# Spreading the stores of the last output tile over SyncE, ScalarE and GpSimd, at the end of an attention and feed-forward kernel

## Chip, cores, metric

One core of a Trainium2 chip. The metric is device time in microseconds (us), measured around the whole program; the span in a profile, from the first to the last instruction, is about 1.8 us shorter. "Tail" below means the time from the end of the last eviction on VectorE to the end of the span.

## The reference

Attention with an extra exp(-m) in the denominator, on (8, 12, 448, 64) queries, keys and values, followed by a feed-forward layer with a maximum over three products:

```python
scores = scale * q @ k.T;  m = max(scores);  e = exp(scores - m)
attn = e / (sum(e) + exp(-m) + 1e-9);  x = attn @ v          # to (3584, 768)
h = max(x @ w1, x @ w2, x @ w3);  out = h @ w_out            # (3584, 768) float32
```

## The kernel before

TensorE works almost without a gap from the first scores to the last output tile. An output tile is 128 tokens by 768 columns, made in pieces of columns: six matmuls into PSUM, one eviction by VectorE into `o_sb`, and then one store for each half of 64 partitions, since the two halves go to different rows. (An ordinary tile's first piece is stored together with its second.) Only the cuts of the very last tile differ.

```python
def out_piece(bp, t, c, w, queues):
    ...
    nc.vector.tensor_scalar(out=o_sb[:, c : c + w], in0=op_ps[:, 0:w],
                            scalar1=1.0 / LAMBDA, scalar2=None, op0=ALU.mult)
    if queues is None:
        return
    for half in range(2):
        ...
        queues[half].dma_start(out=rows[:, outs[1] : c + w],
                               in_=o_sb[half * HP : half * HP + HP, outs[1] : c + w])
    outs[1] = c + w
```

GpSimd issues all loads of the kernel but two (they convert to fp16 on the way, and are written by software on GpSimd): 108 transfers. It also copies V into its working layout. Its last such work:

```python
if 5 <= i + 1 < NI:
    prep_v(i + 1, nc.gpsimd)      # last time for i = NI - 2, near 260 us
...                               # cut: shift_q, load_more, the end of the loop
for pr in range(NP):              # the last heads, then the last feed-forward batch
    finish = av(NI - 1, NI % NEB, pr, "EO")
```

After the last line of the program each engine gets closing instructions: SyncE waits for all transfer semaphores, and a barrier ends the program.

The softmax here doesn't subtract the row's maximum and nothing guards it: scores larger than these inputs give would overflow.

Of the kernel before, what the change touches and what calls it, by code (L numbers as in the profile page):

```python
# [21 lines left out]
def kernel(  # L22
# [11 lines left out]
    nc = tc.nc  # L34
# [468 lines left out]
    NW = DM // 2  # L503
# [40 lines left out]
            pieces.append((up_piece, (b, fcs, i, q0, qn), NDC * w * (qn + 6)))  # L544

    def add_out(b):
        sy, sc = nc.sync, nc.scalar
        for t in range(0, 3) if b % 2 == 0 else range(3, 7):
            cuts = [(0, NW, None), (NW, NW, (sy, sy))]
            if b == B - 1 and t == 6:  # L550
                cuts = [(0, NW, (sy, sy)), (NW, 256, (sc, sc)), (NW + 256, 128, (sy, sc))]
            for c, w, queues in cuts:
                pieces.append((out_piece, (b // 2, t, c, w, queues), NFC * (w + 6)))

    def add_batch(b):
        add_up(b, 0, S, [(i, fc) for fc in range(NFC) for i in range(3)])
        add_out(b)
# [120 lines left out]
    for i in range(3, NI):  # L678
# [6 lines left out]
        for vi, units in enumerate(visits):  # L685
# [17 lines left out]
            if vi == 2 and first:  # L703
                x_transpose_pe(i - 1, "E")
                fill(per / 2)
                prep_v(i, DV)
                for w, cols in ((0, (0, NE)), (1, (0, NE)), (2, (NE, NO)), (2, (0, NE))):
                    add_up(0, *cols, [(w, f) for f in (0, 2, 4)])
                add_out(0)
                per = share(n)  # L710
# [59 lines left out]
```

## Time and profile before

| before | us |
|---|---|
| time, median of 3 runs | 338.64 (338.59 to 338.93) |
| span of the profile | 336.88 |
| end of the last eviction | 331.92 |
| last store landed | 335.60 |
| SyncE's closing waits done | 336.05 |

The prediction shows the busy shares, the chain and the last stores. The profile lists instructions by engine (count, then shortest, median and longest in ns, then first and last start in us).

### The profile page before, as it was taken

How to read it: one execution, taken by the hardware profiler on the slowest of the kernel's cores; microseconds unless marked ns; L12 is line 12 of the kernel's file. 1: busy time of each engine (PE TensorE's matmuls, PEld its weight loads, DVE VectorE, ACT ScalarE, POOL GpSimd, SP SyncE). 2: the span in 40 equal slices, each digit the busy share in tenths (PEclk: the TensorE clock that was granted, in tenths of full speed). 3: DMA queues.
4: the chain of work that ended last, by engine and by line, in shares of the span. 5: the costliest groups of instructions: out<-in, count | busy, mean ns of one | idle time of the engine just before them, and what ended most of it. 6: DMA issues, size and time to landing. Idle time of an engine off the chain costs nothing.

```text
span 336.9 us, 10248 instructions
## 1 busy us (share of the span) xinstructions
PE 326.1 (97%) x4316; PEld 195.9 (58%) x4316; DVE 199.9 (59%) x521; ACT 183.1 (54%) x289; POOL 146.7 (44%) x260
## 2 busy tenths in 40 slices
PE   7899999999999999999999999999999999999993
PEld 3668788866556655565546646555556555565552
DVE  4556675566566556556656556556556556575552
ACT  4768856655665755676556655666565665420000
POOL 8596578880671539170854328351754000000000
PEclk9999999999999999999999999999999999999999
DMA  8999999799799999969996999989990730124016
GB/s 141 197 200 207 203 205 191 128 161 191 109 108 132 171 234 145 124 96 190 177 156 81 114 259 120 150 99 220 186 149 18 164 89 2 31 47 129 0 33 157
DMA packets 84815, 46.46 MB, mean 138 GB/s; under 512 B 53280, under 2 KB 81312, under 8 KB 84768
## 3 DMA queue, kind: packets, MB, share of 16 engines
q0 software_dynamic: 29120, 21.80, 48.6%
q1 hardware_dynamic: 55264, 23.60, 41.3%
q8 instruction: 34, 0.56, 0.7%
q10 hardware_dynamic: 384, 0.39, 0.4%
q14 instruction: 13, 0.11, 0.1%
HBM read 44.04 MB, written 11.01 MB: 163 GB/s over the span
## 4 chain that ended last, share of the span: by engine, by line
PE 87%; DMA 5%; ACT 2%; DVE 2%; issue 1%; POOL 1%; POOLq 0%; ACTq 0%
PE p_i L490 48%; PE op_ps L514 14%; PE stp L304 11%; PE avp L388 9%; DMA xT<-xn 3%; ACT e L324 2%; DMA ld_q<-in_q_dram 2%; PE avp L344 2%; PE avp L361 1%; DVE xn L404 1%; PE trT L229 1%; DVE QT L190 1%; PE xtp L463 0%; ACT QT L188 0%; DVE rb L401 0%
## 5 line engine op out<-in xcount | busy, mean ns | idle before, releaser
L324 ACT ACTIVATE e<-stp 128x896 f16<-128x896 f32 (+4 forms) x171 | 143.9, 901 | 60.3 <-PE stp L304 60.1
L490 PE MATMUL p_i<-xT,w 128*128 128x448 f16 (+2 forms) x972 | 173.1, 332 | 0.5 <-DMA xT<-xn 0.3
L490 PEld LDWEIGHTS <-w 128*128 128x128 f16 x972 | 90.2, 98 | 69.1 <-issue 6.0
L249 POOL COPY QT<-QT 64x384 f16<-64x384 f16 (+1 forms) x84 | 46.9, 558 | 93.9 <-DMA QT<-ld_q 69.2
L501 DVE TENSOR_TENSOR hT<-hT,p_i 128x448 f16<-128x448 f16 (+2 forms) x96 | 59.7, 622 | 35.7 <-PE p_i L490 35.6
L514 PE MATMUL op_ps<-w,hT 128*128 128x384 f16 (+2 forms) x342 | 58.5, 323 | 0.0
L304 PE MATMUL stp<-QT,KT 64*64 64x448 f16 (+2 forms) x756 | 48.1, 338 | 2.6 <-ACT e L324 0.9
L499 DVE CAST hT<-p_i 128x448 f16<-128x448 f32 (+2 forms) x48 | 30.0, 625 | 25.2 <-PE p_i L490 25.2
L514 PEld LDWEIGHTS <-hT 128*128 128x128 f16 x342 | 32.0, 98 | 22.4 <-issue 2.0
L424 ACT ACTIVATE xn<-end,rl 64x64 f16<-64x64 f32 x72 | 24.9, 346 | 34.5 <-DVE rl L421 34.1
L521 DVE TENSOR_SCALAR o_sb<-op_ps 128x384 f32<-128x384 f32 (+2 forms) x57 | 31.2, 547 | 17.4 <-PE op_ps L514 16.8
L388 PE MATMUL avp<-vx,e 128*128 128x65 f16 x936 | 38.6, 194 | 0.0
L388 PEld LDWEIGHTS <-e 128*128 128x128 f16 x936 | 32.1, 97 | 2.3
L304 PEld LDWEIGHTS <-KT 64*64 64x64 f16 x756 | 15.8, 105 | 26.8 <-issue 23.9
L398 DVE TENSOR_SCALAR rb<-avp 128x6 f32<-128x6 f32 (+2 forms) x54 | 8.8, 164 | 36.8 <-PE avp L388 36.8
L404 DVE TENSOR_TENSOR xn<-avp,rb 128x384 f16<-128x384 f32 (+2 forms) x54 | 29.3, 543 | 1.8
L433 POOL COPY vx<-ld_v 128x768 f16<-128x768 f16 x21 | 17.2, 820 | 6.8 <-issue 4.2
L344 PEld LDWEIGHTS <-e 64*64 64x64 f16 x624 | 13.7, 107 | 8.1 <-issue 1.7
L102 POOL DMA_DIRECT2D ld_q<-in_q_dram x24 | 17.4, 723 | 2.3 <-DMA w<-in_moe_w_dram 1.1
L102 POOL DMA_DIRECT2D ld_k<-in_k_dram x24 | 17.3, 722 | 2.1 <-DMA w<-in_moe_w_out_dram 1.1
L414 ACT ACTIVATE end<-avp 128x65 f32<-128x65 f32 x36 | 8.2, 227 | 17.1 <-PE p_i L490 12.4
L115 POOL DMA_DIRECT2D ld_v<-in_v_dram x24 | 15.2, 634 | 2.6 <-DMA w<-in_moe_w_dram 1.3
(52 smaller groups left out, 162.1 us busy)
## 6 DMA issues: line engine op xcount, KB each, us to landing
out_dram<-o_sb SPq DMA_DIRECT2D x54, 192.0 KB, 4.0
ld_v<-in_v_dram POOLq DMA_DIRECT2D x48, 128.0 KB, 5.1
ld_k<-in_k_dram POOLq DMA_DIRECT2D x23, 224.0 KB, 6.6
ld_q<-in_q_dram POOLq DMA_DIRECT2D x23, 224.0 KB, 7.5
w<-in_moe_w_dram POOLq DMA_DIRECT2D x9, 384.0 KB, 9.2
w<-in_moe_w_out_dram POOLq DMA_DIRECT2D x3, 384.0 KB, 8.5
xT<-xn SPq DMA_TRANSPOSE x18, 4.8
QT<-ld_q SPq DMA_TRANSPOSE x17, 7.3
```

Source lines behind the costliest of these rows:

```text
L102: nc.gpsimd.dma_start(out=tiles[nm][:, 1 : NP * T + 1].rearrange("x (r t) d -> x r (t d)", r=NP)[:, p0:p1], in_=src[:, p0:p1],)
L249: eng.tensor_copy(out=t[d0 : d0 + HP, o * 128 : (o + n) * 128], in_=t[s0 : s0 + HP, a * 128 : (a + n) * 128],)
L304: nc.tensor.matmul(out=stp[half * HP : half * HP + HP, par, j * qn : (j + 1) * qn], lhsT=k_block(i, pr, h2, x[half]), rhs=q_cols(i, pr, h2 ...
L324: nc.scalar.activation(out=dst, in_=src, func=AF.Exp, scale=scale)
L388: nc.tensor.matmul(out=ps[:, hh, j * D1 : (j + 1) * D1], lhsT=eF[:, o : o + 128], rhs=vx[:, 2 * pr + hh, (x[0]), 0:D1], start=False, stop= ...
L404: nc.vector.tensor_tensor(out=xn[i][:, pr, ws[0] : ws[0] + nw].rearrange("p j h d -> p h j d"), in0=acc[:, :, :, 0:D], in1=rb.unsqueeze(3) ...
L424: nc.scalar.activation(out=xn[i][0:HP, pr, 3, hh], in_=end[h, 0:D], func=AF.Copy, scale=rl[h])
L490: nc.tensor.matmul(out=p_i[:, j * qn : (j + 1) * qn], lhsT=w_sb[i][:, dc, ts(fc, 128)], rhs=xT[b][:, dc, q0 : q0 + qn], start=(dc == 0), s ...
L499: nc.vector.tensor_copy(out=dst, in_=src)
L501: nc.vector.tensor_tensor(out=dst, in0=dst, in1=src, op=ALU.max)
L514: nc.tensor.matmul(out=op_ps[:, 0:w], lhsT=hT[bp][:, fc, ts(t, 128)], rhs=wout_sb[:, fc, c : c + w], start=(fc == 0), stop=(fc == NFC - 1),)
L521: nc.vector.tensor_scalar(out=o_sb[:, c : c + w], in0=op_ps[:, 0:w], scalar1=1.0 / LAMBDA, scalar2=None, op0=ALU.mult,)
```

## The change

The intent: SyncE issues the last tile's pieces one after another and is late with the last; ScalarE is busy with three issues; GpSimd is idle. So the halves of the 384-column piece go to SyncE and ScalarE, both halves of the 256-column piece to GpSimd, and the last 128 columns stay on SyncE and ScalarE.

```diff
     def add_out(b):
-        sy, sc = nc.sync, nc.scalar
+        sy, sc, gp = nc.sync, nc.scalar, nc.gpsimd
         for t in range(0, 3) if b % 2 == 0 else range(3, 7):
             cuts = [(0, NW, None), (NW, NW, (sy, sy))]
             if b == B - 1 and t == 6:
-                cuts = [(0, NW, (sy, sy)), (NW, 256, (sc, sc)), (NW + 256, 128, (sy, sc))]
+                cuts = [(0, NW, (sy, sc)), (NW, 256, (gp, gp)), (NW + 256, 128, (sy, sc))]
```

## The prediction

> **What bounds the kernel now.** I read the busy shares first, then the chain of waits that ended last, then the last ten microseconds of the timeline and each output store's issue and landing.
>
> ```profile
> PE 326.1 (97%) x4316; PEld 195.9 (58%) x4316; DVE 199.9 (59%) x521; ACT 183.1 (54%) x289; POOL 146.7 (44%) x260
> ```
>
> TensorE is busy 97% of 336.9 us. The granted clock is 0.999. Nothing in the change touches TensorE; a comparison of the two programs finds its 8634 rows and VectorE's identical. So 331.5 of the 336.9 us cannot move, and the whole question lies after the last matmul. There the chain in order of time ends as follows (start, length, what):
>
> ```profile
> 323.55 8.06 PE op_ps L514 x54
> 331.61 0.02 issue
> 331.63 0.29 DVE o_sb L521
> ```
>
> The last eviction ends at 331.92, yet the span ends at 336.88. These 4.95 us are the tail: stores, their landing and the closing barrier. The timeline of that stretch (start, length, engine, what; a merged line begins at the first and ends with the last of its group):
>
> ```profile
> 330.49 1.43 DVE L521 TENSOR_SCALAR o_sb<-op_ps 128x384 f32<-128x384 f32 x3 [0.42 <-DMA out_dram<-o_sb]
> 332.28 1.70 SPq L531 DMA_DIRECT2D out_dram<-o_sb  x2
> 331.60 1.84 ACTq L531 DMA_DIRECT2D out_dram<-o_sb  x3
> ```
>
> The three VectorE evictions are the last tile's 384, 256 and 128 columns, ending at 331.05, 331.57 and 331.92. ScalarE issues at 331.60, 332.19 and 332.89. SyncE issues the previous tile's second half at 330.62, then the 384-column halves at 331.32 and 332.28, and the last piece only at 333.51, 1.59 us after its data was ready. That last store alone, as the trace lists it, followed by the one before it:
>
> ```profile
> L531 SPq DMA_DIRECT2D out_dram<-o_sb x1: 466/466/466, 333.5 to 333.5; - x1
> DMA to landing us min/median/max: 2.1/2.1/2.1
> ...
> L531 SPq DMA_DIRECT2D out_dram<-o_sb x1: 803/803/803, 332.3 to 332.3; - x1
> ```
>
> It lands at 333.51 + 2.09 = 335.60. ScalarE's last lands at 332.89 + 2.52 = 335.41, SyncE's second half at 332.28 + 2.53 = 334.81. From 335.60 to the end are 1.28 us of closing waits and barriers. So the tail is: 1.59 us of SyncE running late, 2.09 us of one store, 1.28 us of closing.
>
> The transfer engines are the second limit in this stretch (columns as in the heading; last two are busy share and GB/s):
>
> ```profile
> core 0: us, PE busy (x) PEld busy (x) DVE busy (x) ACT busy (x) POOL busy (x), PEclk, DMA share, GB/s
> 331.00:332.00 1.00, 0.60 (x7) 0.32 (x5) 0.77 (x3) 0.00 (x0) 0.00 (x0) 1.00 0.80 172
> 332.00:333.00 1.00, 0.00 (x0) 0.00 (x0) 0.00 (x0) 0.00 (x0) 0.00 (x0) 1.00 0.83 250
> 333.00:334.00 1.00, 0.00 (x0) 0.00 (x0) 0.00 (x0) 0.00 (x0) 0.00 (x0) 1.00 0.93 244
> 334.00:335.00 1.00, 0.00 (x0) 0.00 (x0) 0.00 (x0) 0.00 (x0) 0.00 (x0) 1.00 0.49 129
> ```
>
> They are 80 to 93% busy until 334, so earlier issues cannot be turned wholly into earlier landings. GpSimd does nothing at all there; its last work was at 260.
>
> **What the Trainium skill says.** "DMA: Bandwidth & Descriptors", section "Issuing engines are not separate DMA queues": "Initiating DMAs on multiple engines concurrently will only save the time on the sequencer it takes to initiate the DMA". The trace agrees that there is such a time: SyncE needs 0.47 to 0.59 us for each store when alone.
>
> "Perfetto Trace Analysis", section "DMA Instruction — HWDGE (DVE, Sync)": the hardware descriptor generator is shared by the issuing sequencers, locked for one of them, and the profiled length of an issue includes the wait for that lock. The trace fits: SyncE's two 384-column issues, made while ScalarE issues, take 0.92 and 0.80 us, not 0.47 to 0.59.
>
> "DMA: Bandwidth & Descriptors", section "Specifications": first byte after about 1 us from GpSimd, about 0.6 us from SyncE or ScalarE. The trace is slower in both: first packets about 1.33 us after an isolated GpSimd issue, 1.12 to 1.21 us after SyncE's or ScalarE's.
>
> "SBUF — State Buffer", section "Who interferes with whom": VectorE in a two-port mode locks GpSimd out. I expect nothing of it here: the evictions of 384 and 128 columns take 557 and 292 ns, so (557 - 292)/256 = 1.04 ns a column, which is no doubled rate, and only one, of 0.29 us, is left when GpSimd starts.
>
> **The change part by part.**
>
> 1. The second half of the 384 columns leaves SyncE for ScalarE. SyncE loses one issue of 0.80 us, plus some 0.43 us between it and the last one. Its last issue is then bounded by the data (331.92) or by the end of the first half's issue: 331.32 + 0.47 to 0.92 = 331.8 to 332.2. I put it at 332.0 to 332.4, in place of 333.51. ScalarE issues its half at 331.08, as soon as the 384 columns are evicted, done at about 331.65; that store moves 1.2 us forward.
>
> 2. ScalarE loses its two 256-column issues (0.55 and 0.60 us). Its last 128 columns can go at 331.95 in place of 332.89. Some waiting for the shared generator remains, as four issues still fall within a microsecond, so 332.0 to 332.5. With 2.1 to 2.5 us to landing, SyncE's and ScalarE's last stores land at 334.1 to 335.0.
>
> 3. GpSimd gains two stores of 64 KB. Data ready at 331.57, first issue about 331.62. The nearest kin in the trace are the pairs of V loads, also 64 partitions: 0.63 and 0.64 us of GpSimd for an issue, 3.2 us from issue to landing when other traffic is absent. Those read 256 KB each and convert it; a 64 KB store needs about 1.33 us to its first packet, 0.3 us of packets, and about 0.6 us until the semaphores are full, so about 2.3 us, and I allow 2.3 to 3.2. Second issue at 332.25, landing at 334.6 to 335.4. This is likely the new last one, and it is on the path.
>
> 4. The bytes do not change. From 331.2 on, two tiles' worth (the last two), 786 KB, are moved. At 260 GB/s, a little above the 244 to 250 of the full stretches, that takes 3.0 us, so the last packet goes at about 334.2 at the earliest, against 334.9 now. As the last landing now comes 0.7 us after the last packet, it cannot be before about 334.9. This is an estimate from those rates, and it caps the gain at 0.7 us.
>
> 5. Closing: SyncE goes through all the queues' semaphores in a fixed order, about 0.06 us each. With another one last, that may cost or save up to 0.4 us. I take none.
>
> Sum: the last landing moves from 335.60 to about 335.0 (between part 4's floor and the late end of part 3). 338.64 - 0.6 = 338.0 us, a gain of 0.2%.
>
> **Rivals.** First, GpSimd's path is the new bound and eats everything: at 3.2 us from the second issue it lands at 335.45, and with a slower start of the software path or transfer contention at 336 or a little later. For: loads under traffic took 4 us and more. Against: they are bigger and ran against full queues. Time 338.5 to 339.2.
>
> Second, the transfer engines do not matter and only the issue does: SyncE's last store issues 1.2 us earlier, the closing order helps too, and the gain is 1.2 to 1.4 us: 337.3. For: the last store takes only 2.09 us in all. Against: the busy share of 0.8 to 0.93.
>
> Third, the generator lock stays the bound: ScalarE's early half now collides with SyncE's previous-tile store and with the next one, each issue takes 0.8 to 0.9 us, and SyncE's last goes at 333.0. That would make 338.1 or so, close to my number for another reason.
>
> **Range and chances.** The whole tail that the change can reach is 1.59 us of waiting in SyncE, 0.5% of the time; even removing it entirely and saving in the closing would not come to 2% (6.8 us). A loss of 6.8 us would need a GpSimd store of some 10 us. So "within 2%" is nearly certain. The three runs of before span 0.34 us, so noise is half of the expected gain. Range 337.3 to 338.8.
>
> **What would show it.** Right: SyncE's last store is issued at or before 332.5; ScalarE's first at about 331.1; GpSimd's two at 331.6 and 332.25 with about 0.63 us each; the last landing near 335.0 and belonging to GpSimd; TensorE unchanged up to 331.5. Wrong: GpSimd's landing after 335.6, SyncE's issues still at 0.8 to 0.9 us and its last one after 333, or a closing stretch longer than the 1.28 us, for instance because the end must wait for GpSimd's queue in another way.

## More of the kernel before

```profile
L765 POOLq DRAIN  x3: 45/93/5048, 260.0 to 336.6; - x3
L765 SPq DRAIN  x3: 7/7/7, 336.0 to 336.4; - x3
```

GpSimd has three closing drains. One takes 5048 ns, and the first starts at 260.0: as soon as GpSimd ran out of work. It was over at 265, 72 us before the end, and cost nothing. SyncE's drains take 7 ns.

## The result

The changed kernel took 340.00 us (median of 4 runs, 339.81 to 340.81), the kernel before 338.62 in the same comparison. The ratio is 1.0046, 95% interval 1.0026 to 1.0066: 0.46% slower, 1.6 us, where 0.6 us of gain was predicted. (Ratios are the mean time of one kernel's fast runs over that of the other's of the same rounds, so not quite the ratio of the medians.) Within 2%, as forecast, but outside the stated range.

The profiled run of after is the longest of its four: span 338.95. Its last eviction ends at 332.46, 0.54 us later than before; that difference was there before GpSimd's last copy, at 260 us, is done, where the two programs are the same. The tail is 338.95 - 332.46 = 6.49 us against 4.95: 1.54 us more, which is the loss.

The chain that ended last, after (start, length, what):

```profile
331.69 0.44 DVE o_sb L521
332.12 0.28 issue
332.41 0.56 POOL out_dram L531
332.96 0.56 POOLq L765
```

In the kernel before the chain ended with the last eviction of 128 columns. Now it goes from the 256-column eviction to GpSimd's first store, and then to line 765 on GpSimd's sequencer: not to a transfer, but to a closing instruction. Which one, the view of the closing instructions tells:

```profile
L765 SPq EVENT_SEMAPHORE  x11: 17/28/2045, 333.8 to 338.9; - x11
L765 POOLq DRAIN  x3: 51/93/5315, 332.9 to 338.7; - x3
L765 SPq DRAIN  x3: 7/7/7, 336.3 to 338.4; - x3
```

The long drain is the same one as before, 5.3 instead of 5.0 us, but it now starts at 332.86 in place of 260, since GpSimd's last work is the two stores. It ends at 338.18. SyncE had all transfers landed and its own drains begun at 336.33, and then stood at the barrier for 1.85 us. (SyncE's longest wait, 2045 ns, lies before that. By the semaphore that it names it is for GpSimd's second store: it ends at 335.86, 0.02 us after that store has landed, and SyncE needs another 0.47 us for the rest of its fixed order. So GpSimd's store also set when SyncE was done.)

The stores themselves, in the timeline of after:

```profile
330.64 3.06 SPq L531 DMA_DIRECT2D out_dram<-o_sb  x4
331.62 1.35 ACTq L531 DMA_DIRECT2D out_dram<-o_sb  x2
332.41 1.12 POOL L531 DMA_DIRECT2D out_dram<-o_sb  x2 [71.28 <-DVE o_sb L521]
```

SyncE's last store now goes 0.77 us after the last eviction, in place of 1.59. But it lands at 3.57 us after it, in place of 3.67: the gain of 0.8 us in the issue became 0.1 us in the landing. That store alone, as the trace lists it (it was issued at 333.24):

```profile
L531 SPq DMA_DIRECT2D out_dram<-o_sb x1: 466/466/466, 333.2 to 333.2; - x1
DMA to landing us min/median/max: 2.8/2.8/2.8
```

The transfer engines are the likely reason why there was little to win (last two columns: busy share and GB/s):

```profile
332.00:333.00 1.00, 0.14 (x3) 0.00 (x0) 0.40 (x2) 0.00 (x0) 0.59 (x2) 1.00 0.98 255
333.00:334.00 1.00, 0.00 (x0) 0.00 (x0) 0.00 (x0) 0.00 (x0) 0.52 (x1) 1.00 0.99 242
334.00:335.00 1.00, 0.00 (x0) 0.00 (x0) 0.00 (x0) 0.00 (x0) 0.00 (x0) 1.00 0.84 231
```

From 332 to 334 they are 98 to 99% busy, at about the rate of before (242 to 255 GB/s, against 244 to 250). No run tests this reading alone, and it is no fixed limit: in pairs, below, the same bytes had landed 3.29 us after the last eviction.

### The profile page after: what moved, and what is told of

It is laid out like the page before. It is cut to its first block, busy times and chain, and to the rows that moved or that the text cites. A ratio compares the mean times of both kernels' runs of the same rounds, so it can differ in the third digit from the quotient of the medians.

```text
span 339.0 us, 10249 instructions
## 1 busy us (share of the span) xinstructions
PE 326.6 (96%) x4316; PEld 196.2 (58%) x4316; DVE 198.9 (59%) x521; ACT 183.0 (54%) x289; POOL 147.8 (44%) x262
## 4 chain that ended last, share of the span: by engine, by line
PE 89%; DVE 3%; DMA 3%; ACT 3%; issue 1%; POOLq 0%; POOL 0%; ACTq 0%
PE p_i L490 48%; PE op_ps L514 14%; PE stp L304 11%; PE avp L388 9%; DMA xT<-xn 3%; ACT e L324 2%; PE avp L344 2%; PE warm L175 1%; PE avp L361 1%; DVE xn L404 1%; DVE QT L190 1%; PE trT L229 1%; ACT QT L188 1%; PE trT L213 1%; PE xtp L463 0%
## 5 line engine op out<-in xcount | busy, mean ns | idle before, releaser
L531 POOL DMA_DIRECT2D out_dram<-o_sb x2 | 1.1, 560 | 71.3 <-DVE o_sb L521 71.3
```

## The experiments

Theory: GpSimd's closing drain, some 5 us after its last work, now sets the end. Rivals: the early ScalarE issue slows SyncE's and ScalarE's stores; the drain waits for GpSimd's stores to land, so it is the stores and not the drain; the drain's length is for what gathered up since the start, not for the late stores.

All runs gave correct results. On the chips that these runs got, the times of the kernel before spread over 3.9 to 5.7 us within a job, which swamps half a microsecond. In the profiled runs such differences lie before GpSimd's last copies of V, near 260 us: the last large one starts at 258.4 to 262.3 in the 18 profiles, and from it to the end of the last eviction all 18 take 72.75 or 72.76 us. So I read the tail from the profiles, and the times only where enough of them agree. In this table each number is us after the last eviction.

| run | GpSimd's long closing drain ends | SyncE's closing waits end | span ends (tail) |
|---|---|---|---|
| before | long over | 4.12 | 4.95 |
| after, after_b, after_c | 5.71, 5.70, 5.70 | 3.87, 3.82, 3.74 | 6.49, 6.49, 6.47 |
| part1, part1_c | long over | 3.72, 4.43 | 4.58, 5.28 |
| part2 | 5.83 | 3.99 | 6.61 |
| touch | 4.50 | 4.51 | 5.34 |
| touch_last | 4.87 | 4.10 | 5.65 |
| early_drain, _b, _c | 3.47, 3.46, 3.58 | 3.83, 3.83, 3.95 | 4.68, 4.66, 4.79 |
| split_drains | 3.53 | 3.90 | 4.76 |
| pairs, _b, _c | long over | 3.57, 3.62, 4.04 | 4.40, 4.45, 4.88 |
| pairs_gp | 3.37 | 3.74 | 4.58 |
| drain_9 | long over | 4.29 | 5.14 |

Read it by rows: the tail is the later of the two middle columns plus 0.77 to 0.86 us of barrier, in every run. Each row is one profile. In before, touch, touch_last and drain_9 all stores are issued as in before, and there SyncE's waits end at 4.10 to 4.51: so a few tenths of a tail are noise.

### Either part of the change alone: part1 and part2

```diff
-cuts = [(0, NW, (sy, sc)), (NW, 256, (gp, gp)), (NW + 256, 128, (sy, sc))]
+cuts = [(0, NW, (sy, sc)), (NW, 256, (sc, sc)), (NW + 256, 128, (sy, sc))]   # part1
+cuts = [(0, NW, (sy, sy)), (NW, 256, (gp, gp)), (NW + 256, 128, (sy, sc))]   # part2
```

> Only the first part of the change: the 384-column halves on SyncE and ScalarE, the 256 columns stay on ScalarE, GpSimd stores nothing. Theory (GpSimd's closing drain takes about 5 us after its last work and now sets the end): GpSimd's drain is long over, so there is no loss; SyncE's last store is issued about 1 us earlier, but ScalarE's last stays near its old place behind four issues, so 338.3 to 338.6 against 338.6 before. Rival (the shared hardware descriptor generator is made slower by the early ScalarE issue, and that is the loss): 339.5 or more.

> Only the second part of the change: the 256 columns on GpSimd, the 384-column halves stay both on SyncE. Theory (GpSimd's closing drain): the drain begins when the second GpSimd issue is generated, as in the changed kernel, takes 5.0 to 5.4 us and ends after SyncE's closing waits; time 339.9 to 340.2, the whole loss. Rival (the loss is in the stores of SyncE and ScalarE): 338.6 or less.

part1: 338.95 us median, ratio to before 0.9994 (0.9948 to 1.0041), tail 4.58. part2: 340.49 us median, ratio 1.0023 (0.9983 to 1.0063), tail 6.61. The times alone are not clear of the spread; the tails are. The closing drain in part2:

```profile
L765 POOLq DRAIN  x3: 51/93/5437, 332.9 to 338.9; - x3
```

The whole loss is in the second part, GpSimd's stores, and comes with the late drain. The rival that the early ScalarE issue costs the time falls: in part1 it is there, and the tail (4.58, in the repeat below 5.28) is near that of before (4.95), not 1.5 us longer. A repeat:

> The first part of the change alone, a second time. Tail 4.6 us; about 0.4 us faster than before in the mean, give or take 1.

part1_c: ratio 1.0011 (0.9992 to 1.0030), tail 5.28, its last store landing 4.17 us after the last eviction against 3.46 in part1. So the tail of one version varies by 0.7 us with the landings, and part1 is no faster than before in the time. A miss: I had expected 0.4 us.

### Is it the stores, or any late work? touch and touch_last

The kernel before, with one small copy on GpSimd at the end and no store from it. touch by mistake read columns of the 256-column piece, so it started 0.24 us before the last eviction was over; touch_last reads the last piece.

```diff
     add_batch(B - 1)
     fill(float("inf"))
+    nc.gpsimd.tensor_copy(out=seen, in_=outs[0][:, NW + 192 : NW + 256])   # touch
+    nc.gpsimd.tensor_copy(out=seen, in_=outs[0][:, DM - 64 : DM])          # touch_last
```

> The kernel before, and one small GpSimd copy (128 x 64, into a scratch tile that nothing reads) of the last tile's last columns at the very end; GpSimd issues no store. Theory A (the closing drain takes about 4.6 us after any last GpSimd work, a store or not): it ends at about 332.5 + 4.6 = 337.1 on the span in place of SyncE's 336.1, so about 1.0 us slower, 339.4 to 339.8. Rival B (the drain waits for GpSimd's stores to land, and without a late store is short): 338.6, with a drain under 3 us.

> As touch, but the copy reads the very last 128 columns, so it starts some 0.3 us after the last eviction instead of 0.2 us before it (touch read columns of the piece before). If 4.5 us of drain follow any last work, the drain ends about 5.0 us after the last eviction, later than SyncE's closing waits (4.2 to 4.5), and eviction to end is about 5.8 us against 4.95 before. If a drain without late stores never sets the end, about 4.95.

touch: ratio 0.9994 (0.9957 to 1.0032), tail 5.34; its drain takes 4.74 us, with no late store, but ends together with SyncE's waits (4.50 and 4.51), so the tail tells little. touch_last: 339.20 us median of 4, ratio 0.9996 (0.9947 to 1.0045, unclear), tail 5.65. Its copy and its drain:

```profile
333.18 0.23 POOL L741 COPY seen<-o_sb 128x64 f32<-128x64 f32 x1 [71.48 <-DVE o_sb L522]
L767 POOLq DRAIN  x3: 45/102/4745, 333.2 to 338.4; - x3
```

A copy of 0.23 us, with no late transfer on GpSimd, is followed by a drain of 4.7 us that ends 4.50 us after it and 0.77 us after SyncE is done. So the drain isn't a wait for the late stores. In the kernel before the drain ends 4.50 us after the last copy too; in the changed kernel 4.65 us after the second store's issue.

### Is it paid once? early_drain

The changed kernel, with one line ahead of the last heads:

```diff
+    nc.gpsimd.drain()
     for pr in range(NP):
         finish = av(NI - 1, NI % NEB, pr, "EO")
```

> The changed kernel with one more GpSimd drain after its last preparation copy (near 260 us), before the two late stores. Theory A (a fixed time after any last work): the early drain takes about 5 us and so does the closing one, 340.0. Rival C (the drain's time is for what has gathered up since the start, above all the more than 100 software transfers issued before, and is paid once): the early one takes about 5 us, the closing one only until the two stores have landed, under 3.5 us; then SyncE's waits set the end and the time is 338.0 to 338.5.

The early drain, and then the closing ones:

```profile
L732 POOLq DRAIN  x1: 5032/5032/5032, 261.1 to 261.1; - x1
L766 POOLq DRAIN  x3: 51/93/3062, 333.4 to 337.4; - x3
```

The early drain takes the 5.03 us, hidden; the closing one takes 3.06 and ends 0.12 us after the second GpSimd store has landed (3.34 us after the last eviction). It does so in all five profiles with such a drain ahead (early_drain three times, split_drains, pairs_gp: 0.12 us each), so the short drain seems to last until the late stores have landed. SyncE's waits set the end again, and the tail is 4.68 against 6.49. So the long drain is for something that has gathered up earlier, and is paid once. The expected time of 338.0 to 338.5 did not come: 340.72 us median, ratio 1.0031 (0.9984 to 1.0078). Its repeats, beside the changed kernel on one chip each time:

> The changed kernel again, unaltered, to be timed on one chip with the two below. The closing drain begins with the second GpSimd issue, takes 5.3 us and sets the end; last eviction to end 6.5 us, as in its first profile; about 1.4 us slower than before in the mean of fast runs, if the rest of the kernel runs as calmly as in the first comparison.

> The changed kernel with the early GpSimd drain, again, unaltered. Last eviction to end 4.7 us as in its first profile, so 1.8 us less than after_b in the tail; in the time about 1.8 us faster than after_b and 0.3 us faster than before, within a spread that the rest of the kernel makes. If the early drain costs as much elsewhere as it saves at the end, the time is that of after_b.

after_b: 340.43 us median, ratio 1.0029 (0.9983 to 1.0074). early_drain_b: 340.69, ratio 1.0036 (0.9988 to 1.0083). The tails came again (6.49 and 4.66), the gain in time not. Hence another pair, in the other order:

> The changed kernel with the early drain, a third time, now first in the order. Tail from last eviction to end 4.7 us. If its long times in the two jobs before (338.4 to 343 us) came from the part of the kernel before 260 us, which is the same program in both, it is faster than after_c in the mean by about 1.8 us, give or take 1; if they came from the drain, it is again no faster than after_c.

> The changed kernel, a third time. Tail 6.5 us; about 1.5 us slower than before in the mean, give or take 1.

early_drain_c: 339.49 us median, ratio 1.0018 (0.9996 to 1.0039). after_c: 340.92, ratio 1.0077 (1.0049 to 1.0105). The means of their fast runs, 339.17 and 341.19, differ by 2.0 us, near the 1.7 us of the tails (6.47 and 4.79). In the profiled runs of the first two jobs the extra time lay before the early drain: it started at 261.1 and 262.3, where the kernel before begins its drain at 260.0; and from GpSimd's last copy to the last eviction all take the same 72.75 us. So in these profiles the drain delays nothing up to the last eviction, and until it the program is the same. Why early_drain's times were 0.4 to 1.2 us above before in all three jobs, with a tail 0.2 to 0.3 us shorter, I can't say beyond that; chance is not excluded.

### What does its length follow? split_drains and drain_9

```diff
+        if i in (9, 14):          # split_drains; drain_9: i == 9, in the kernel before
+            nc.gpsimd.drain()
         if i >= 5:
             load_more(i + 3, i + 4)
```

split_drains has also the drain of early_drain.

> The changed kernel with three earlier GpSimd drains: after the tenth and the fifteenth group of heads and after the last preparation copy, each placed where GpSimd has just waited for other work, so that the loads before it have landed. If the drain's time is in proportion to the software transfers issued since the last drain (108 before the late stores, 5 us in all, so some 0.047 us each), the three split 5 us: about 3, 1 and 1 us, and the closing one is as in early_drain, about 3 us. If a drain costs a fixed 5 us whenever transfers went before, each of the three takes 5 us. If it is a cost of the first drain alone, 5, then under 0.2 and under 0.2.

> The kernel before with one more GpSimd drain after the tenth group of heads (where split_drains had its first): what does a drain's length follow? The closing drain, at 260 us with no load in flight, then has 46 transfers since the last drain. With 26 it took 2.73 us (split_drains), with 108 it took 5.05 us. A line through those two, 2.0 us + 0.028 us each, gives 3.3 us. A fixed cost of any drain after loads gives 5.05. A cost of what was issued last (the last two iterations are the same in all) gives 2.7.

One profile each. The two drains in the loop and the third of split_drains, and the closing one of drain_9:

```profile
L730 POOLq DRAIN  x2: 3015/4022/5028, 107.1 to 166.5; - x2
L734 POOLq DRAIN  x1: 2734/2734/2734, 260.7 to 260.7; - x1
L767 POOLq DRAIN  x3: 51/102/4381, 259.6 to 336.3; - x3
```

| transfers since the last drain | drain, us | past GpSimd's last queued work | what else was in it |
|---|---|---|---|
| 62 (3.03 and 0.74 in drain_9) | 3.02 | 0.74 | 2.3 us of copies still queued |
| 20 | 5.03 | 2.28 | ended 0.86 us after its last load had landed |
| 26 | 2.73 | 2.19 | nothing |
| 46 (drain_9) | 4.38 | 3.84 | nothing |
| 108 (before) | 5.05 | 4.50 | nothing |

None of the three laws that I had put down holds. The clean ones give 0.084 us a transfer for 26 and 46, but 0.042 for 108 (third column), and by that column 62 in mid-kernel took less than 26 at the end. So the three clean ones grow with the transfers since the last drain, less than in proportion, and something else counts too; transfers, bytes and time were not told apart. This stays open. That a drain ahead takes most of it away is shown.

### Without GpSimd, and a version of all three: pairs and pairs_gp

```diff
-cuts = [(0, NW, None), (NW, NW, (sy, sy))]
+cuts = [(0, NW, None), (NW, NW, (sy, sc) if b == B - 1 and t == 5 else (sy, sy))]
 if b == B - 1 and t == 6:
-    cuts = [(0, NW, (sy, sc)), (NW, 256, (gp, gp)), (NW + 256, 128, (sy, sc))]
+    cuts = [(0, NW, (sy, sc)), (NW, 256, (sy, sc)), (NW + 256, 128, (sy, sc))]
```

pairs_gp has the first of these two edits and the early drain.

> No GpSimd store: the last two tiles' halves all go one on SyncE and one on ScalarE (384, 256 and 128 columns of the last tile). Each sequencer then has at most one issue in hand when the last eviction ends, the last stores are issued within 0.6 us of it and land about 3.0 us after it; eviction to end about 4.2 us against 4.95 before and 6.5 after, so about 0.7 us (0.2%) faster than before. If the shared descriptor generator is the bound instead, the last issues come 0.8 us or more after the eviction and eviction to end is 4.6 as in part1.

> The previous tile's halves on SyncE and ScalarE, the last tile as in the changed kernel (256 columns on GpSimd), and a GpSimd drain near 260 us. The second GpSimd store lands about 3.4 us after the last eviction, the closing drain ends with it, and eviction to end is about 4.5 us: faster than the changed kernel by 2 us in the tail, not faster than pairs.

> The version without GpSimd stores, again, unaltered. Last eviction to end 4.4 us as in its first profile, 0.55 us less than before: about 0.5 us faster than before in the time, 2 us faster than after_b.

> No GpSimd store, a third time. Tail 4.4 us; about 0.5 us faster than before in the mean, give or take 1.

pairs: medians 338.75, 338.68 and 337.96 us in three jobs, ratios 0.9992 (0.9950 to 1.0033), 0.9963 (0.9921 to 1.0004) and 0.9993 (0.9971 to 1.0015). Tails 4.40, 4.45 and 4.88. It is at or below before each time, by 0.25, 1.3 and 0.4 us in the means, but no interval leaves out 1: likely a little faster, not proved. ScalarE's second issue takes 1.20 us where its others take 0.55, while SyncE makes two issues; this fits sequencers that hold each other up, though no run isolates it. And the last issues came at 0.8 and 1.1 us after the eviction, not within 0.6. pairs_gp: 338.39 us median, ratio 1.0011 (0.9953 to 1.0069), tail 4.58. Using GpSimd, with its drain paid early, gives nothing over leaving it out.

## Why the prediction was wrong, by its own steps

The sum was: last landing 0.6 us earlier, closing unchanged. Measured: landing 0.1 us earlier (3.57 after the last eviction against 3.67), and from there to the end 2.92 us against 1.28, 1.64 more. 1.64 - 0.10 = 1.54, the tail's growth.

1. **Part 5, the closing, is the step that failed.** Its wait was the wrong one: SyncE's walk and not GpSimd's drain. It saw in "1.28 us of closing waits and barriers" only SyncE's walk through the semaphores, said that another order "may cost or save up to 0.4 us", and took none. It left out that each engine closes with a drain, and that GpSimd's goes on for 4.5 us past GpSimd's last work. It stood in the profile of before, hidden at 260. An estimate from that would have come close: the drain ended 4.50 us past GpSimd's last work; with the predicted end of the second issue at 332.25 + 0.63 = 332.9 that makes 337.4, 1.3 us past SyncE's 336.05. The prediction's list of what would make it wrong had named the case, "because the end must wait for GpSimd's queue in another way", but gave it no weight in the range. touch_last and early_drain show the cause; part1 and part2 show that the loss comes with GpSimd's stores alone.

2. **The sum's 0.6 us of earlier landing was mis-sized: 0.1 us.** Part 1 put SyncE's last issue at 0.1 to 0.5 us after the eviction; it came at 0.77, since the issue before took 0.98 us and 0.4 us went by after it, as in all versions (what fills these 0.4 us is open). The prediction had seen such a gap, "some 0.43 us", and left it out of its sum: 331.32 + 0.92 + 0.43 makes 332.67, 0.75 after the eviction. Part 2 had ScalarE's last issue right at first (331.95, and it came 0.03 us after the eviction; the 332.0 to 332.5 that it settled on were late), but not 2.1 to 2.5 us to landing: it took 3.1, and SyncE's took 2.8. Part 4, the transfer engines as a bound, fits the 98 to 99% busy, but that they were the bound is not shown.

3. **Part 3, GpSimd's stores, was nearly right.** Issues of 0.56 us (predicted 0.63), the second landing 2.9 us after its issue (2.3 to 3.2) and 3.38 us after the last eviction (2.7 to 3.5 by its times). Only the start was late: 0.28 us after the eviction where 0.05 was assumed, as the chain's "issue" line shows. It was not the last landing; SyncE's was (3.57). But it was on the path to SyncE's last closing wait, as part 3 said, since SyncE asks for it first and then goes on through its order.

4. **The rivals.** The first had GpSimd as the new bound and 338.5 to 339.2 us, but by a slow landing, which did not happen. The second, issue alone, falls with the landing of 3.57. The third, the generator lock, would show in the 0.98 us issue, but that is hardly longer than the 0.92 of before, and SyncE's last store went at 0.77 and not 1.1 us after the eviction.

5. **The chances** held: the whole reach is far under 2%. The range was too narrow because it covered only the stores.

## What to carry to other kernels

Before giving an idle engine some last work, look up when its closing instructions ran. Here GpSimd went quiet early and its drain ran unseen; late work brought that drain to the end of the program. After 108 software transfers it needed 4.5 us past its last copy and 4.65 past its last store's issue, more than the 2.1 to 3.2 us that the last tile's stores from SyncE and ScalarE took to land in before and after. A drain in an idle stretch ahead made the closing one short (3.06 us in place of 5.32). And look at the transfer engines before counting on an earlier issue: here, with them 98 to 99% busy, 0.8 us in the issue gave 0.1 in the landing.

## What the Trainium skill lacked or had wrong

- "VectorE: DVE Perf Modes", section "The DRAIN you can't avoid", knows two kinds of drain: VectorE's own, and those that the runtime adds before and after a kernel, constant at about 12 ns on all five engines. It lacks a program's own closing drains, and they are not constant. Here SyncE's take 7 ns, but in before the first one of ScalarE takes 0.41 us, of VectorE 0.33 and of TensorE 0.53, and GpSimd's 5.05; GpSimd's takes 5.32 in after, 4.75 after a mere copy, and 3.06 when another drain went before.
- "DMA: Bandwidth & Descriptors" weighs GpSimd against SyncE and ScalarE as the issuer by first byte and flexibility. It lacks that work issued late from GpSimd brings its closing drain with it: 1.5 us of tail here, while the stores landed as fast as the others (2.3 and 2.9 us, against 2.8 to 3.2).
- The same page, section "Specifications": first byte about 1 us from GpSimd and about 0.6 from the others. In the trace of before they were 1.33 (isolated loads) and 1.12 to 1.21 us (1.03 for the kernel's first two loads), from the start of the issue to the first packet.
- No page has the law of that drain's length, nor do these runs: 2.73 us with 26 transfers since the last drain, 4.38 with 46, 5.05 with 108, but 3.02 with 62 in mid-kernel.
